# The low product of P moved behind the transposes of the next block, in attention with a two-layer FFN on one NeuronCore

## The chip, the cores and the metric

The kernel runs on one core of a Trainium2 chip. The metric is the device time of one execution in microseconds; the median of the runs counts. Names used below: PE is TensorE, DVE is VectorE, ACT is ScalarE, POOL is GpSimd, SP is SyncE, which issues all the DMAs.

## The reference

Inputs are q, k, v of 8 batches x 12 heads x 448 positions x 64, two vectors of gains, and the weights w_in (768 x 2048) and w_out (2048 x 768).

```
q_n, k_n = rmsnorm(q, g_q), rmsnorm(k, g_k)
attn = softmax(q_n @ k_n.T / sqrt(64))          # per batch and head, 448 x 448
x = (attn @ v) as 3584 x 768                    # heads side by side
h = x @ w_in
out = (h * cos(h)) @ w_out
```

## The kernel before, in words

Two heads of a batch make a unit: 48 units, `u` from 0 to 47. Units 0 to 5 (`u < NP`, called plain in the code) compute in float32. All others split their operands into a high part in the rounded type float32r and a low part, the rest, and add up the products high x high, low x high and so on, so that each product of 448 columns goes through PE in the faster type.

One unit from the seventh on goes like this.
- Scores: seven tiles of 128 queries, two or three matmuls each (`score`, L568). DVE scales and takes the row minimum (`rowmin`, L572), ACT takes the exponential and writes P, unnormalised, to SBUF (`expo`, L580). P has 11 slots of 448 columns; slots 0, 1 and 5 are used by every unit, the others by every second one.
- P has to be turned before it can be multiplied by v. `transp` does this on PE, in four blocks of keys, `kc` 0 to 3. Blocks 0 to 2 have two groups of transposes each, `part` 0 with four tiles into PSUM bank PT0 and `part` 1 with three tiles into PT1 (L614). Block 3 has 64 keys left for each head; three transposes (L619) turn a joint piece of both heads and one more (L621) turns tile 3, all into PT0, in one group. With block 1 goes a small transpose of the reciprocal row sums (L623).
- `pt_high` (ACT, L637) casts the bank to float32r, `hi`; `pt_low` (DVE, L644) subtracts and writes `lo`. In block 3 the low part goes into the other 64 partitions of `hi` (L646), so one product does both.
- `av` on PE multiplies for each of the two heads `hh`: the high product (L661) has as weights the high and the low part of v side by side, 128 columns; the low product (L663) has the high part of v alone, 64 columns. Both add to the PSUM bank `O{hh}` of the unit, which block 0 opens and block 3 closes.
- ACT and DVE copy and add the two halves of O (`x_half`, `x_sum`), POOL normalises (`x_norm`), and the result is split in high and low for the FFN.

The first FFN layer of a batch (`ffn1`, L745 to L747, six matmuls to a part, 48 parts for a batch) runs on PE between the attention of the next batch. Behind the attention comes the second layer (`ffn2`, L819 to L821), with some 470 us of its own.

The order of the work is planned when the kernel is built. Each piece is registered with `add(engine, cost, due, function, ..., r=keys read, w=keys written)`. The planner runs the pieces by their costs; on each engine, of the pieces whose inputs are there, the one with the smallest due time comes next. `dk` is the due time of a block, four units of planner time apart; a table shifts the due times by function (transposes of part 0 by -4.1, of part 1 by +2.4, `av` by +5.3). The costs only set the order. On the chip each engine works through its list in that order, and semaphores hold it where an input is missing. Keys such as `("lo", ...)`, `("pt", 0, half)` and `("O0", u)` stand for tiles and banks; `RING` gives how many buffers each name has: two each for `hi` and `lo`, one each for O0 and O1.

The product of a block in the code before, high and low one behind the other:

```
        nc.tensor.matmul(O, st, d["hi", kc][:, HEADS[hh]], start=(kc == 0), stop=(kc == 3))
        if kc < 3:
            nc.tensor.matmul(O[:D], vs[:, 0], d["lo", kc][:, HEADS[hh]], start=False, stop=False, skip_group_check=True)
```

Of the kernel before, what the change touches and what calls it, by code (L numbers as in the profile page):

```python
# [20 lines left out]
PE, ACT, DVE, POOL, SP = "PE", "ACT", "DVE", "POOL", "SP"  # L21
# [147 lines left out]
def tile_attention_moe(  # L169
# [11 lines left out]
    nc = tc.nc  # L181
    NU = sd_in.shape[0]
    B, S, D = 8, kq_in.shape[2] - 512, 64
    NP = NU // B
    NQT = 7
    NVC = 4
# [102 lines left out]
    stage, quad, part = {}, {}, {}  # L289
# [45 lines left out]
    pair = {}  # L335
# [20 lines left out]
    def p_key(u, t):  # L356
        slot = SLOTS[u % 2][TURNED[u % 2].index(t)]
        return (f"P{slot}", u if slot in (0, 1, 5) else u // 2)

    def p_slot(key):  # L360
        return int(key[0][1:])

    def p_rows(u, t):
        return pbuf[:, p_slot(p_key(u, t))]
# [236 lines left out]
    pt = [ps_t.tile([128, 512], F32, tag=f"PT{i}", name=f"PT{i}") for i in range(2)]  # L601
    TILES = ((0, 1, 2, 3), (4, 5, 6))
    COLS = (slice(0, 512), slice(512, 896))
    WIDE = (512, 384)
    HEADS = (slice(0, S), slice(S, 2 * S))
# [3 lines left out]
    def transp(u, kc, part, last):  # L609
        k = KS[kc]  # L610
        if kc < 3:
            for i, t in enumerate(TILES[part]):
                c = k + 64 * (t > 3)
                nc.tensor.transpose(pt[part][:, i * 128 : i * 128 + 128], p_rows(u, t)[:, c : c + 128], ident)  # L614
        else:
            flat = pbuf.rearrange("p n s -> p (n s)")
            for t in range(3):
                e = S * (p_slot(p_key(u, t)) + 1)
                nc.tensor.transpose(pt[0][:, t * 128 : t * 128 + 128], flat[:, e - 64 : e + 64], ident)  # L619
            c, n = (k - 64, 128) if u < NP else (k, 64)  # L620
            nc.tensor.transpose(pt[0][:n, 384:512], p_rows(u, 3)[:, c : c + n], ident)  # L621
        if last:
            nc.tensor.transpose(pt[1][:NQT, 384:512], pair[u]["sm"][:, 3, :], ident)  # L623

    def p_tile(u, kc, name, dt, part):
        if part == 0:
# [21 lines left out]
    def o_bank(u, hh):  # L648
        return pair[u]["O", hh]

    def o_open(u, hh):
        pair[u]["O", hh] = ps_o.tile([128, 512], F32, tag=f"O{hh}", name=f"O{u}_{hh}")

    def av(u, kc, hh):
        d = pair[u]
        if kc == 0:
            o_open(u, hh)
        O = o_bank(u, hh)[:, :S]
        vs = d["vs"][:, hh * NVC + kc]
        st = vs.rearrange("p a d -> p (a d)")  # L660
        nc.tensor.matmul(O, st, d["hi", kc][:, HEADS[hh]], start=(kc == 0), stop=(kc == 3))  # L661
        if kc < 3:
            nc.tensor.matmul(O[:D], vs[:, 0], d["lo", kc][:, HEADS[hh]], start=False, stop=False, skip_group_check=True)  # L663

    def pt_copy(u, kc, part):
        p = p_tile(u, kc, "hi", F32, part)
# [337 lines left out]
    def attend(u):  # L1004
        D0 = base(u)
        b, cc = divmod(u, NP)
        plain = u < NP
        step = 3.0 if plain else 4.0
        lead = 0.0 if u < NP else None
        def soften(t, n, key, due):  # L1010
            add(DVE, 0.65, due, rowmin, u, t, r=[("r", u)], w=[key, ("sm", u, 1, t)])
            add(ACT, 0.65, due + 1, expo, u, t, r=[key, ("sm", u, 1, t)], w=[p_key(u, t), ("sm", u, 2, t)])

        for j in range(4):
            if not plain:
                break
            tiles = (3,) if j == 3 else (j, j + 4)
            keys = [place(u, 2 * j + n) for n in range(len(tiles))]
            dj = D0 + step * j
            add(PE, 1.1 if j < 3 else 0.92, dj, score_plain, u, j, lead=lead, r=[("qp", u), km_key(u), ("xsb", 0)], w=keys)  # L1020
            for n, t in enumerate(tiles):
                soften(t, 2 * j + n, keys[n], dj + 1)
        for n, t in enumerate(TURNED[u % 2]):
            if plain:
                break
            key, dj = place(u, n), D0 + 0.5 * step * n
            if t == 3:
                r = [("qhi", u), ("ql", u), ("khi", u), ("kl", u)]
            else:
                r = [("D", u), ("E", u), ("M", u, 0), ("M", u, 1)]  # L1030
            add(PE, 0.62 if t == 3 else 0.41, dj, score, u, n, lead=lead, r=r, w=[key])
            soften(t, n, key, dj + 1)
        D1 = D0 + 4 * step
        add(ACT, 0.2, D1, rsum, u, 0, r=[("sm", u, 2, t) for t in range(7)], w=[("sm", u, 3)])
        add(DVE, 0.2, D1 + 1, rsum, u, 1, w=[("sm", u, 3)])
        for n, kc in enumerate((0, 1, 3, 2) if plain else range(4)):
            dk = D1 + step * n
            m = 4 * u + n
            turn = kc == KTURN
            for half in range(1 + (kc < 3)):  # L1040
                r = [p_key(u, t) for t in (TILES[half] if kc < 3 else range(7))]
                w = [("pt", 0, half)]
                last = turn and half == 1
                if last:
                    r.append(("sm", u, 3))
                if half and kc in (KTURN, KTURN + 1):
                    w.append(("pt", 0, 2))
                cost = (0.47, 0.36 + 0.11 * last)[half]
                add(PE, cost, dk, transp, u, kc, half, last, r=r, w=w, lead=lead)
            lows = []  # L1050
            for half in range(2):
                bank = ("pt", 0, half if kc < 3 else 0)
                keys = dict(r=[bank], w=[("hi", m, half)])
                if plain:
                    if kc < 3 or not half:
                        add((ACT, DVE)[half], (0.49, 0.42)[half], dk + 1, pt_copy, u, kc, half, **keys)
                else:
                    add(ACT, (0.52, 0.43)[half], dk + 1, pt_high, u, kc, half, **keys)
                if turn and half:
                    add(DVE, 0.28, dk + 1, rs_copy, u, r=[("pt", 0, 2), ("hi", m, 1)], w=[("rt", u)])  # L1060
                    add(SP, ISS, dk + 2, rs_store, u, r=[("rt", u)], w=[("rsd", u)], kb=4.0)
                if not plain:
                    l = 3 * u + kc
                    r, w = [bank], [("hi", m, half)]
                    if kc < 3:
                        r, w = r + w, [("lo", l, half)]
                    lows.append((half, r, w))
            for half, r, w in lows:
                if kc == 3:
                    r = r + [("hi", m, 1)]  # L1070
                add(DVE, (0.64, 0.5)[half], dk + 2, pt_low, u, kc, half, r=r, w=w)
            for hh in range(2):
                r = [("hi", m, half) for half in range(hh + 1)]
                if plain:
                    if kc < 3:
                        add(PE, 0.88, dk + 3, av_plain, u, kc, hh, lead=lead, r=[("vs", u)] + r, w=[(f"O{hh}", u)])
                    elif not hh:
                        add(PE, 1.3, dk + 3, av_plain, u, kc, hh, lead=lead, r=[("vs", u)] + r, w=[("O0", u), ("O1", u)])
                    continue
                if kc < 3:  # L1080
                    r += [("lo", l, half) for half in range(hh + 1)]
                add(PE, 0.41 if kc < 3 else 0.21, dk + 4, av, u, kc, hh, lead=lead, r=[("vs", u)] + r, w=[(f"O{hh}", u)])
        D2 = D1 + 4 * step + 1
        add(SP, 2 * ISS, D1 + 9, rs_load, u, r=[("rsd", u)], w=[("rs", u)], kb=224.0)
        for hh in range(2):
            if plain:
                add(DVE if hh else ACT, 0.55, D2, x_plain, u, hh, r=[(f"O{hh}", u)], w=[("xf", u, hh)])
                continue
            add(ACT, 0.54, D2, x_half, u, hh, r=[(f"O{hh}", u)], w=[("xf", u, hh)])
            add(DVE, 0.62, D2 + 1, x_sum, u, hh, r=[(f"O{hh}", u)], w=[("xf", u, hh)])  # L1090
        x = [("xf", u, 0), ("xf", u, 1)]
        add(POOL, 1.22, D2 + 5, x_norm, u, r=[("rs", u)], w=x)
        add(ACT, 0.46, ffn_due(b, 0) - 6, x_split, u, 0, r=x + ([] if b else [('xsb', 1)]), w=[("xs", cc, 0)])
        add(POOL, 1.11, ffn_due(b, 0) - 5, x_split, u, 1, r=x + [("xs", cc, 0)], w=[("xs", cc, 1)])
# [68 lines left out]
    add = plan.add  # L1163
# [3 lines left out]
    for fc in range(NEAR, NFC):  # L1167
        n = fc - NEAR
        d, y, he = BLOCK * n, ("y", n % 8), (("he", "he2")[n % 2], n // 2)
# [32 lines left out]
    for t in range(B // 2):  # L1202
# [26 lines left out]
        for k, (name, q, w0, bk, opens, closes) in enumerate(PRODUCTS):  # L1229
            d = DUE[name]  # L1230
# [5 lines left out]
            for g in range(NGR):  # L1236
# [6 lines left out]
                for o in range(3):  # L1243
                    add(PE, BLOCK / 3, e + BLOCK / 3 * o, ffn2, n, g, wpos, role[bk][o], o, opens,
                        r=[hk, lk] + [("wp", i) for i in wpos], w=[("y", role[bk][o])])
# [88 lines left out]
```

## Time and profile before

| | |
|---|---|
| median of 3 runs | 1373.1 us (1373.09 to 1374.74) |
| span of the profiled execution, first to last instruction | 1369.6 us |
| the execution's own time beside its span | not given by itself; the median of the runs is 3.5 us above the span |
| busy time in the span: PE, DVE, ACT, POOL | 1343.3, 1074.6, 926.7, 631.4 us |
| first and last low product (L663) | 109.5 and 889.5 us |

The profile is one execution on the chip. Times are microseconds, those marked ns nanoseconds. PE is the matmuls of TensorE, PEld its weight loads, which can overlap them. The start of a matmul is recorded, its end is modelled, and matmuls are pipelined, so an instruction of 0.37 us can be followed by the next one 0.20 us later. In an instruction's form, 128*64 means that 128 rows and 64 columns of the array are in use, that is, weights with 64 columns. L663 is line 663 of the kernel. An arrow names what ended the idle time before an instruction.

### The profile page before, as it was taken

What the parts mean: (1) busy time and instruction counts of PE and PEld (TensorE: products, weight loads), DVE (VectorE), ACT (ScalarE), POOL (GpSimd) and SP (SyncE); (2) the same over time, 40 slices, a digit from 0 to 9 for tenths busy, and PEclk for the clock granted to TensorE, in tenths of its full rate; (3) what the DMA queues carried; (4) which work ended last, traced back from release to release, by engine and by line L of the source; (5) the groups of instructions that cost most, each with busy time, mean ns of one, the idle gap of its engine ahead of it and who ended that gap; (6) DMA issues with size and microseconds to landing.
All of it is one profiled execution on the core that took longest, in us unless ns stands there. A gap on an engine that the chain in (4) does not pass through costs nothing.

```text
span 1369.6 us, 21501 instructions
## 1 busy us (share of the span) xinstructions
PE 1343.3 (98%) x6998; PEld 1172.3 (86%) x6998; DVE 1074.6 (78%) x1859; ACT 926.7 (68%) x1872; POOL 631.4 (46%) x554
## 2 busy tenths in 40 slices
PE   7899999999999999999999999999999999999998
PEld 3347888788888989888889888999999999999998
DVE  7898999977787887777877877628889889889743
ACT  6677888777877877777777787638567366366321
POOL 4889978676766866766776584330000000000000
PEclk9999999999999999999999999999999999999999
DMA  6898777889797898798987897338988368369334
GB/s 240 268 280 180 197 167 200 231 233 243 202 263 205 224 241 209 213 244 231 240 211 197 226 234 199 121 126 315 375 295 301 120 245 308 112 247 313 105 113 153
DMA packets 149472, 302.19 MB, mean 221 GB/s; under 512 B 34368, under 2 KB 83088, under 8 KB 149360
## 3 DMA queue, kind: packets, MB, share of 16 engines
q1 hardware_dynamic: 149360, 300.83, 75.4%
q8 instruction: 55, 0.90, 0.3%
q14 instruction: 57, 0.47, 0.1%
HBM read 193.99 MB, written 62.73 MB: 187 GB/s over the span
## 4 chain that ended last, share of the span: by engine, by line
PE 83%; DVE 6%; POOL 4%; DMA 3%; issue 2%; ACT 2%; SPq 0%; POOLq 0%; ACTq 0%; DVEq 0%
PE y L820 10%; PE y L819 10%; PE y L821 10%; PE ph L745 8%; PE ph L746 8%; PE ph L747 8%; PE S L568 7%; PE PT L614 6%; PE O L661 4%; PE O L663 3%; DVE S L572 1%; PE O L679 1%; PE S L552 1%; DVE lo L644 1%; PE y L747 1%
## 5 line engine op out<-in xcount | busy, mean ns | idle before, releaser
L572 DVE TENSOR_SCALAR_CACHE_REDUCE S<-S,r 128x448 f32<-128x448 f32 x336 | 225.2, 686 | 56.1 <-PE S L568 47.0
L580 ACT ACTIVATE P<-S,sm 128x448 f32<-128x448 f32 x336 | 213.4, 638 | 73.8 <-DVE S L572 56.3
L745 PE MATMUL ph<-xs,wi 128*128 128x448 f32 x660 | 251.1, 381 | 0.4 <-ACT hbuf L763 0.2
L819 PE MATMUL y<-g,wo 128*128 128x448 f32 x672 | 245.4, 365 | 0.0
L820 PE MATMUL y<-g,wo 128*128 128x448 f32 x672 | 245.4, 365 | 0.0
L821 PE MATMUL y<-g,wo 128*128 128x448 f32 x672 | 245.4, 365 | 0.0
L746 PE MATMUL ph<-xs,wi 128*128 128x448 f32 x660 | 241.8, 366 | 0.0
L747 PE MATMUL ph<-xs,wi 128*128 128x448 f32 x660 | 241.3, 366 | 0.0
L801 ACT CAST g<-gq 128x896 fp32r<-128x896 f32 x112 | 105.6, 943 | 169.8 <-PE y L821 169.4
L637 ACT CAST hi<-PT 128x512 fp32r<-128x512 f32 (+2 forms) x336 | 175.8, 533 | 64.1 <-PE PT L614 22.4
L644 DVE TENSOR_TENSOR lo<-PT,hi 128x512 fp32r<-128x512 f32 (+1 forms) x252 | 153.2, 619 | 39.7 <-ACT hi L637 37.6
L799 DVE TENSOR_TENSOR g<-gq,g 128x896 fp32r<-128x896 f32 x112 | 121.9, 1089 | 59.7 <-ACT g L801 59.2
L614 PEld LDWEIGHTS PT<-ident,P 128*128 128x128 f32 x1008 | 124.1, 141 | 41.9 <-issue 6.2
L614 PE MATMUL PT<-ident,P 128*128 128x128 f32 x1008 | 155.6, 275 | 2.9 <-DVE lo L644 1.2
L745 PEld LDWEIGHTS ph<-xs,wi 128*128 128x128 f32 x660 | 124.3, 188 | 16.4 <-ACT hbuf L763 2.0
L820 PEld LDWEIGHTS y<-g,wo 128*128 128x128 f32 x672 | 126.2, 188 | 10.0
L819 PEld LDWEIGHTS y<-g,wo 128*128 128x128 f32 x672 | 126.2, 188 | 9.9
L821 PEld LDWEIGHTS y<-g,wo 128*128 128x128 f32 x672 | 126.2, 188 | 9.9
L747 PEld LDWEIGHTS ph<-xs,wi 128*128 128x128 f32 x660 | 124.0, 188 | 10.6
L746 PEld LDWEIGHTS ph<-xs,wi 128*128 128x128 f32 x660 | 124.5, 189 | 8.7
L400 POOL TENSOR_TENSOR r<-r,nhalf 128x14 f32<-128x14 f32 (+1 forms) x48 | 124.1, 2586 | 4.0
L661 PE MATMUL O<-hi,vs 128*128 128x448 f32 x336 | 122.6, 379 | 1.1 <-DVE hi L646 0.9
(129 smaller groups left out, 2636.0 us busy)
## 6 DMA issues: line engine op xcount, KB each, us to landing
wo<-wo_d SPq DMA_DIRECT2D x152, 384.0 KB
gq<-h_d SPq DMA_DIRECT2D x64, 448.0 KB
h_d<-hbuf SPq DMA_DIRECT2D x54, 448.0 KB
wo_d<-ao SPq DMA_DIRECT2D x56, 384.0 KB
sd<-sd SPq DMA_DIRECT2D x46, 448.0 KB
kq<-kq SPq DMA_DIRECT2D x42, 480.0 KB
D<-qhi SPq DMA_DIRECT2D x84, 192.0 KB
raw<-w_in SPq DMA_DIRECT2D x16, 768.0 KB
```

The costliest lines, as they stand in the source:

```text
L572: nc.vector.tensor_scalar(d["S", t][:, :S], d["S", t][:, :S], d["r"][:, t : t + 1], None, op0=ALU.mult, op1=ALU.min, accum_out=d["sm"][:, ...
L580: nc.scalar.activation(p_rows(u, t), d.pop(("S", t))[:, :S], AF.Exp, bias=sm[:, 1, t : t + 1], scale=-1.0, accum_out=sm[:, 2, t : t + 1],)
L614: nc.tensor.transpose(pt[part][:, i * 128 : i * 128 + 128], p_rows(u, t)[:, c : c + 128], ident)
L637: nc.scalar.copy(hi if kc < 3 else hi[:64], pt_rows(u, kc, part))
L644: nc.vector.tensor_tensor(lo, src, hi.bitcast(F32), ALU.subtract)
L661: nc.tensor.matmul(O, st, d["hi", kc][:, HEADS[hh]], start=(kc == 0), stop=(kc == 3))
L745: nc.tensor.matmul(ph[:, :S], whi, x2[:, 0, :], start=(cc == 0), stop=False)
L746: nc.tensor.matmul(ph[:, :S], whi, x2[:, 1, :], start=False, stop=False)
L747: nc.tensor.matmul(ph[:, :S], wlo, x2[:, 0, :], start=False, stop=(cc == NCC - 1))
L819: nc.tensor.matmul(y, whi, hi[:, e], start=first and e == 0, stop=False, **more)
L820: nc.tensor.matmul(y, whi, lo[:, e], start=False, stop=False, **more)
L821: nc.tensor.matmul(y, wlo, hi[:, e], start=False, stop=last and e == NG - 1, **more)
```

## The change

The low product leaves `av`. It is issued as `av_low` at the end of `transp`: the group `part` of block `kc` ends with the low product of block `kc - 1` for head `part`. For block 3 `transp` is therefore called twice: part 0 has the three joint transposes, part 1 the transpose of tile 3, and each ends with a low product of block 2. The planner is told that these groups read `lo` of the block before and write the bank O, and gets new costs for them and for `av`. The first six units and their calls stay as they are.

```
-        else:
+        elif part == 0:
             flat = pbuf.rearrange("p n s -> p (n s)")
             for t in range(3):
...
+        if kc == 3 and (part or u < NP):
             c, n = (k - 64, 128) if u < NP else (k, 64)
             nc.tensor.transpose(pt[0][:n, 384:512], p_rows(u, 3)[:, c : c + n], ident)
         if last:
             nc.tensor.transpose(pt[1][:NQT, 384:512], pair[u]["sm"][:, 3, :], ident)
+        if u >= NP and kc:
+            av_low(u, kc - 1, part)
...
         nc.tensor.matmul(O, st, d["hi", kc][:, HEADS[hh]], start=(kc == 0), stop=(kc == 3))
-        if kc < 3:
-            nc.tensor.matmul(O[:D], vs[:, 0], d["lo", kc][:, HEADS[hh]], start=False, stop=False, skip_group_check=True)
+
+    def av_low(u, kc, hh):
+        vh = pair[u]["vs"][:, hh * NVC + kc, 0]
+        O = o_bank(u, hh)[:D, :S]
+        nc.tensor.matmul(O, vh, pair[u]["lo", kc][:, HEADS[hh]], start=False, stop=False, skip_group_check=True)
...
-            for half in range(1 + (kc < 3)):
-                r = [p_key(u, t) for t in (TILES[half] if kc < 3 else range(7))]
-                w = [("pt", 0, half)]
+            for half in range(1 + (kc < 3 or not plain)):
+                tiles = TILES[half] if kc < 3 else range(7) if plain else ((0, 1, 2, 4, 5, 6), (3,))[half]
+                r = [p_key(u, t) for t in tiles]
+                w = [("pt", 0, half if kc < 3 else 0)]
+                if kc and not plain:
+                    r += [("vs", u)] + [("lo", 3 * u + kc - 1, h) for h in range(half + 1)]
+                    w.append((f"O{half}", u))
...
                 cost = (0.47, 0.36 + 0.11 * last)[half]
+                if not plain and kc:
+                    cost = (0.43, 0.33 + 0.11 * last)[half] if kc < 3 else (0.32, 0.11)[half]
+                    cost += 0.15
                 add(PE, cost, dk, transp, u, kc, half, last, r=r, w=w, lead=lead)
...
-                if kc < 3:
-                    r += [("lo", l, half) for half in range(hh + 1)]
-                add(PE, 0.41 if kc < 3 else 0.21, dk + 4, av, u, kc, hh, lead=lead, r=[("vs", u)] + r, w=[(f"O{hh}", u)])
+                add(PE, 0.205, dk + 4, av, u, kc, hh, lead=lead, r=[("vs", u)] + r, w=[(f"O{hh}", u)])
```

## Rows read from the trace of the kernel before

**Rows 1.** The page: the span, and the chain that ended last by engine.
```profile
span 1369.6 us, 21501 instructions
...
PE 83%; DVE 6%; POOL 4%; DMA 3%; issue 2%; ACT 2%; SPq 0%; POOLq 0%; ACTq 0%; DVEq 0%
```
**Rows 2.** Stretches: length, busy time of the engines, granted clock, DMA share, GB/s.
```profile
100.00:250.00 150.00, 144.66 (x772) 122.83 (x771) 136.22 (x250) 118.32 (x268) 130.50 (x107) 0.99 0.76 188
250.00:895.00 645.00, 641.80 (x3549) 573.41 (x3548) 501.03 (x1067) 491.88 (x1153) 420.38 (x375) 1.00 0.83 218
895.00:1369.60 474.60, 470.74 (x2323) 435.99 (x2321) 353.78 (x368) 246.34 (x292) 9.58 (x9) 1.00 0.64 225
```
**Rows 3.** Groups by line and form: count, busy us, mean ns, idle before, releaser.
```profile
L663 PE MATMUL O<-lo,vs 128*64 128x448 f32 x252 | 92.7, 368 | 1.4 <-DVE lo L644 1.4
L661 PEld LDWEIGHTS O<-hi,vs 128*128 128x128 f32 x336 | 61.6, 189 | 12.5 <-DVE hi L646 1.7 <-issue 0.6 <-ACT sd L391 0.5
L663 PEld LDWEIGHTS O<-lo,vs 128*64 128x64 f32 x252 | 34.0, 135 | 5.7 <-DVE lo L644 2.1
```
**Rows 4.** One stretch, L663 alone: length, busy us of PE and PEld (count), clock, DMA.
```profile
100.00:250.00 150.00, 16.65 (x44) 6.10 (x44) 0.99 0.76 188
```
**Rows 5.** Timeline of PE, steady flow: start, duration, line, tiles, form, count.
```profile
499.76 0.37 PE L663 MATMUL O<-lo,vs 128*64 128x448 f32 x1
499.97 0.36 PE L661 MATMUL O<-hi,vs 128*128 128x448 f32 x1
500.17 0.37 PE L663 MATMUL O<-lo,vs 128*64 128x448 f32 x1
```
**Rows 6.** Timeline of weight loads behind a group of transposes.
```profile
503.26 0.19 PEld L745 LDWEIGHTS ph<-xs,wi 128*128 128x128 f32 x1
503.37 0.19 PEld L746 LDWEIGHTS ph<-xs,wi 128*128 128x128 f32 x1
```
**Rows 7.** Timeline of PE at the same place.
```profile
503.26 0.27 PE L614 MATMUL PT<-ident,P 128*128 128x128 f32 x1
503.29 0.45 PE L745 MATMUL ph<-xs,wi 128*128 128x448 f32 x1
503.58 0.36 PE L746 MATMUL ph<-xs,wi 128*128 128x448 f32 x1
```
**Rows 8.** Timeline of weight loads behind an idle gap.
```profile
117.62 0.19 PEld L568 LDWEIGHTS S<-M,D 128*128 128x128 f32 x1 [1.24 <-ACT P L580]
117.73 0.19 PEld L568 LDWEIGHTS S<-M,E 128*128 128x128 f32 x1
```
**Rows 9.** Timeline of PE behind two idle gaps, with 128 and with 64 columns.
```profile
117.62 0.47 PE L568 MATMUL S<-M,D 128*128 128x448 f32 x1 [1.00 <-ACT P L580]
117.93 0.37 PE L568 MATMUL S<-M,E 128*128 128x448 f32 x1
...
139.90 0.42 PE L663 MATMUL O<-lo,vs 128*64 128x448 f32 x1 [0.37 <-DVE lo L644]
140.16 0.49 PE L619 MATMUL PT<-ident,P 128*128 128x128 f32 x3
```
**Rows 10.** Timeline of weight loads within transposes, one of them with 64 columns.
```profile
513.43 0.11 PEld L621 LDWEIGHTS PT<-ident,P 128*64 128x64 f32 x1
513.54 0.36 PEld L614 LDWEIGHTS PT<-ident,P 128*128 128x128 f32 x3
```
**Rows 11.** Timeline of PE in one unit: transposes of blocks 2 and 3, a product.
```profile
491.82 0.60 PE L614 MATMUL PT<-ident,P 128*128 128x128 f32 x4
492.17 0.45 PE L661 MATMUL O<-hi,vs 128*128 128x448 f32 x1
...
495.45 0.49 PE L619 MATMUL PT<-ident,P 128*128 128x128 f32 x3
```
**Rows 12.** Timeline of weight loads in the float32 units, transposes and then L679.
```profile
68.63 0.14 PEld L614 LDWEIGHTS PT<-ident,P 128*128 128x128 f32 x1
68.94 0.19 PEld L679 LDWEIGHTS O<-hi,vs 128*64 128x64 f32 x2 [0.17 <-issue]
```

## The prediction

> **What bounds the kernel now.** I read the page first, then the stretches, then single instructions of TensorE. The page gives TensorE 83% of the chain that ended last, over a span of 1369.6 us [rows 1]; the reader should see that no other engine holds more than 6% of that chain. The stretches split this up [rows 2]: from 250 to 895 us TensorE is idle for 645.0 - 641.8 = 3.2 us, from 100 to 250 us for 150.0 - 144.7 = 5.3 us, and behind 895 us, where no product of P is left, for 3.9 us. The granted clock is 1.00 from 250 us on, so the upper of the two levels. VectorE and ScalarE have 501 and 492 of the 645 us. So between 100 and 895 us the time is the sum of the slots that TensorE's instructions take, one behind the other, plus at most 8.5 us of idle time. The change lies wholly in that part. A busy TensorE is not a TensorE at its peak, though, and the question is how long a slot is.
>
> A slot is the distance between two starts. In steady flow it is 0.20 to 0.21 us for a product of 448 columns, whether its weights have 64 columns (low part, L663) or 128 (L661) [rows 5]. A weight load lasts 189 ns for 128 columns and 135 ns for 64 [rows 3]; in steady flow it runs under the product before it, and the 54 ns of difference are worth nothing.
>
> **Where they could be worth something: behind a transpose.** A transpose takes only 0.11 us [rows 10]. Behind the last one of a group the weights of the next product start to load at 503.26 us, and the load behind that one can start only 0.11 us later, at 503.37 [rows 6]. The product itself was taken up at 503.29, 0.03 us behind the start of that load, and its successor came at 503.58, 0.29 us later and not 0.20 [rows 7]. That looks like a product that stands ready and waits for its weights. A place where nothing else can have been waited for gives the same numbers: after an idle gap the load at 117.62 us is followed by the next at 117.73, 0.11 us again [rows 8], and from its product to the next it is 117.93 - 117.62 = 0.31 us. The low product behind an idle gap (139.90, after a wait for VectorE) has 140.16 - 139.90 = 0.26 us, and the instruction lasts 0.42 us, not 0.47 [rows 9]. So a product with 64 columns of weights whose load is bare is 0.05 us shorter than one with 128.
>
> **The change, part by part.** Each of the 42 units from the seventh on has three blocks with a low product for two heads: 252 products [rows 3]. None is added or removed; the count of matmuls, loads, casts and transfers stays, and no DMA and no work of GpSimd or SyncE is moved past another by hand.
> - The low product moves from behind its high product to behind a group of transposes. There its load is bare, and it is the short one. Before, five of these six groups of a unit ended in a 128-column load (the last block had one group, now two). I take 0.05 us for each of the 252 places, the difference just read: 252 x 0.05 = 12.6 us. Bounds: 0 if the transpose itself and not the load holds the array for those 0.11 us (rival 1), 0.054 us by the durations of the loads [rows 3], 13.6 us.
> - The Trainium skill says in "TensorE: Matmul & The Clock Gate", section "LDWEIGHTS (loading the stationary operand)", that a load takes its columns divided by 1.2 in ns, which is 107 and 53. The bare load of 0.11 us agrees with the first; by that rule the sum would be an estimated 13.4 us.
> - The product behind the low one, formerly bare behind transposes, now loads under 0.20 us of product: no cost.
> - 44 of the 252 lie between 100 and 250 us (7.3 units at six each) [rows 4], where TensorE idles for other reasons and a shorter slot partly turns into more idle time. I count these by half: 22 x 0.05 = 1.1 us less, 11.5 us.
> - The wait for the low part (VectorE, L644) leaves the product. It is 1.4 us in all [rows 3]. The transposes of the next block had to wait for the same subtraction before, because they overwrite the bank it reads. So nothing new is waited for there; up to 1.4 us might go. I set this to nothing against the next item.
> - New order: the transposes of a block now come behind the high product of the block before, since both write the same O bank. Before, the first high product of a unit's block 0 stood at 492.17 us, behind the transposes of block 2 (491.82), and those of block 3 came at 495.45 [rows 11]. Block 1 must now come behind that product, so the transposes of blocks 1 to 3 slide back by more than one distance between blocks, 495.45 - 491.82 = 3.6 us. Queued behind them are casts, subtractions, and the exponentials of the next unit, which share three slots of P with this one. The cover is that TensorE has FFN products to fill with: idle time is 0.5% of the stretch from 250 us on. I set it to nothing; if the cover fails it is rival 2.
> - The split of the last block into two groups moves one transpose by at most one product; the cast of that block waits 0.2 us longer, under FFN products.
>
> The profiled execution spans 1369.6 us; the median of the three runs is 1373.1, and I take the 3.5 us between them as lying around the span and unchanged. Sum: 1369.6 - 11.5 + 3.5 = 1361.6 us. Work behind 895 us comes earlier and is no shorter.
>
> **The rivals.**
> 1. *The transpose holds the array.* From one transpose to the next it is 0.11 us even where the next weights have 64 columns: the load at 513.43 is followed by another at 513.54 [rows 10]. That speaks for an array that is occupied for 0.11 us whatever is loaded, and then the short load gains nothing. Against it: the FFN product was taken up 0.03 us behind the start of the last transpose [rows 7], where a following transpose is not. Only the 1.4 us of waits and about half of the 3.2 us of idle time are left to gain: 1370 to 1373.1 us.
> 2. *The new order starves TensorE (slower).* Place: the transposes of blocks 1 to 3 and the exponentials behind them. Price: where the units don't yet cover each other, from 100 to 250 us, TensorE loses 5.3 us in 7.3 units [rows 2, 4], 0.73 us each; at that rate 42 units lose 31 us, and 1361.6 + 31 is about 1392 us. It decides from 11.5 / 42 = 0.27 us a unit on. For it speaks that the order is set by due times that stay as they are; against it, that the FFN products fill 99.5% of the later stretch now.
> 3. *Going from 128-column to 64-column weights empties the array (slower).* A product of the first six units (L679, 64 columns, plain float32 operands) shows this behind transposes: its load starts at 68.94 us, 0.31 us behind that of the last transpose at 68.63, with 0.17 us idle [rows 12], where steady flow has 0.11. It is 0.20 us late; less the 0.05 us that the short load may give back this is 0.15 to 0.20 us at 252 places, 38 to 50 us: 1411 to 1423 us. The Trainium skill has the rule, "TensorEngine Tiling (Array Packing)", section "Key Properties": a change of tiling mode drains the engine. Against it: L661 and L663 alternate now between 128 and 64 columns at 0.20 to 0.21 us with no gap [rows 5], so the low product does not seem to switch anything.
>
> **How the numbers follow.** My forecast 0.64; rival 1 0.18; rival 2 0.11; rival 3 0.07. The predicted time is that of the likeliest: 1361.6 us. Its own range is 1355 (13.6 us, the 1.4 us of waits and the 3.2 us of idle time all gone) to 1367 (half lost to the new order). The whole range adds rival 1 and stops short of 2 and 3, which hold 0.18: 1354 to 1375 us. Runs of this kernel differ by 0.1%, and 0.2%, 2.7 us, is about what can be told from no change. Forecast and the better edge of rival 1 (0.04) are faster: 0.68. The rest of rival 1 is no change: 0.14. Rivals 2 and 3 are slower: 0.18.
>
> **What would show it.** In the profile after, the low product directly behind a transpose should have its successor 0.26 us after the start of its load (0.31 under rival 1; a gap before its load under rival 3). TensorE's idle time from 250 to 895 us should stay below 6 us; over 15 us says rival 2, and then the waits will name P, hi or S. The last product of attention, now before 895 us, should come some 11 us earlier and the stretch behind it keep its length. The prediction is wrong if either the slot is not shorter or the idle time grows by as much as it is.

## The result and the profile after

The kernel with the change takes 1387.6 us (median of 4 runs, 1385.4 to 1393.1), the kernel before, run beside it, 1373.1 us (4 runs, 1372.4 to 1374.7). The ratio is 1.0112, with a 95% interval of 1.009 to 1.0133: slower, where 1361.6 us and faster had been forecast. The span of the profiled execution grew from 1369.6 to 1385.7 us, by 16.1 us. The medians are only 14.5 us apart: a run takes some 2 us more than its span, so the traced execution of the kernel before was about 1.6 us shorter than the median. (The prediction had put all 3.5 us between the two around the span.)

The page of the kernel after: the span, and the chain that ended last, by engine.

```profile
span 1385.7 us, 21559 instructions
...
PE 79%; DMA 6%; POOL 4%; ACT 4%; DVE 3%; issue 2%; SPq 1%; POOLq 0%; ACTq 0%; DVEq 0%
```

Against [rows 1] TensorE lost four points of the chain, DMA gained three and ScalarE two. The stretches of the kernel after (columns as in [rows 2]; the last row is a narrower look at the place where the second layer begins):

```profile
100.00:250.00 150.00, 142.48 (x752) 120.52 (x751) 134.17 (x248) 116.87 (x266) 124.84 (x104) 0.99 0.73 183
250.00:895.00 645.00, 640.03 (x3524) 574.99 (x3522) 503.99 (x1054) 484.90 (x1143) 422.40 (x372) 1.00 0.85 216
...
960.00:985.00 25.00, 20.27 (x88) 17.93 (x87) 22.88 (x24) 17.72 (x25) 0.00 (x0) 0.86 0.86 305
```

The reader should look at the count as well as at the busy time. TensorE's idle time from 250 to 895 us grew by only 1.8 us (5.0 for 3.2), and from 100 to 250 us by 2.2 us; but 25 and 20 matmuls fewer were started in these stretches. The ends of matmuls are modelled, and an instruction is recorded as longer than its slot, so a wait shorter than some 0.16 us (0.37 of duration less 0.20 of slot) is not seen as idle time at all, and of every longer wait the first 0.16 us are missing.

A measure that sees it: for each matmul, the distance of its end from the end of the one before, less 0.203 us for a product of 448 columns or 0.109 us for a transpose (the slots of steady flow), summed from 110 us (where the plain float32 units are over) to the last product of attention. This **lost time in attention** is 19.2 us before and 27.6 us after. What grew are the longer waits: the places that lose more than 0.16 us add up to 15.1 us before (31 places) and 24.5 us after (51); in both kernels the slots of 3.4 us at the lower clock are among them.

With it the 16.1 us divide as follows.
- The last product of attention ends at 903.9 us instead of 892.7: 11.2 us later. Of this 8.4 us are lost time, and 2.2 us are first-layer work done earlier (from that product to the second layer it is 62.1 us instead of 64.3, so this part comes back). The remaining 0.6 us lie before 110 us.
- The second layer, from its first product to the end, takes 419.7 us instead of 412.6: 7.1 us more. At its start stands a stall that wasn't there before. Timeline of TensorE after, at that place:

```profile
971.53 0.74 PE L825 MATMUL y<-g,wo 128*128 128x448 f32 x1 [4.63 <-DMA wo<-wo_d]
972.07 0.57 PE L826 MATMUL y<-g,wo 128*128 128x448 f32 x1
972.44 0.57 PE L827 MATMUL y<-g,wo 128*128 128x448 f32 x1
...
976.55 0.47 PE L826 MATMUL y<-g,wo 128*128 128x448 f32 x1
976.86 0.37 PE L827 MATMUL y<-g,wo 128*128 128x448 f32 x1
```

  TensorE waits 4.63 us for weights of the second layer, and behind that its slots are 0.37 us instead of 0.20: the granted clock is at 0.5, the lower of its two levels, from 969.9 to 976.8 us (mean 0.86 in the window row above); it fell within the wait. Wait and clock together lose 7.3 us.

Why were the weights late? They are unpacked on the chip, split into two parts and stored (`v_store`, L332) in spare time during attention, and loaded again for the second layer. SyncE's queue, last stores and then the loads of `gq`, first before:

```profile
916.73 4.31 SPq L332 DMA_DIRECT2D wo_d<-ao  x2
...
921.13 4.69 SPq L776 DMA_DIRECT2D gq<-h_d  x9
```

and after:

```profile
924.25 17.03 SPq L332 DMA_DIRECT2D wo_d<-ao  x5
941.37 5.30 SPq L782 DMA_DIRECT2D gq<-h_d  x9
```

The last store starts at 941.0 us, 37.0 us behind the last product of attention, where before it was at 920.7, 28.0 us behind it (the rows give the stretch of several stores, which ends 0.3 us later). The first load of these weights follows at 949.8 us, before at 928.7. When attention ends, seven of the stores are still to come, where before there were four. The small jobs that lead to them have late due times and run between other work; what made them later in this order was not traced.

**The low product itself.** Timeline of TensorE after, at a block of the unit of [rows 11]:

```profile
492.01 0.60 PE L614 MATMUL PT<-ident,P 128*128 128x128 f32 x4
492.36 0.45 PE L669 MATMUL O<-lo,vs 128*64 128x448 f32 x1
492.65 0.36 PE L751 MATMUL ph<-xs,wi 128*128 128x448 f32 x1
```

and its weight loads:

```profile
492.34 0.14 PEld L669 LDWEIGHTS O<-lo,vs 128*64 128x64 f32 x1
492.45 0.19 PEld L751 LDWEIGHTS ph<-xs,wi 128*128 128x128 f32 x1
492.65 0.19 PEld L752 LDWEIGHTS ph<-xs,wi 128*128 128x128 f32 x1
```

The successor comes 492.65 - 492.34 = 0.31 us behind the start of the low product's load, not the forecast 0.26. That is the figure of rival 1, and the same 0.29 us from product to product as with 128 columns [rows 7]. There is no gap ahead of the load either, as rival 3 would have had it.

**Who waits.** Waits of TensorE (total us, times, longest), one of before, then after:

```profile
PE ph L745 <- ACT hbuf L763: 0.2, 1, 0.2
```

```profile
PE ph L751 <- ACT hbuf L769: 4.7, 8, 2.1
PE y L825 <- DMA wo<-wo_d: 4.6, 1, 4.6
...
PE O L664 <- DVE hi L649: 1.4, 2, 1.1
PE O L664 <- ACT hi L640: 1.2, 4, 0.5
```

Waits of ScalarE before, then after (its list is worked through in order, so what stands behind a waiting cast waits with it):

```profile
ACT P L580 <- DVE S L572: 56.3, 69, 2.6
ACT hi L637 <- PE PT L614: 22.4, 34, 1.8
ACT hi L637 <- PE O L661: 21.5, 25, 2.2
ACT hbuf L763 <- PE ph L747: 18.9, 38, 1.6
...
ACT P L580 <- PE PT L619: 11.8, 9, 1.9
```

```profile
ACT hi L640 <- PE PT L614: 45.0, 44, 3.4
ACT hbuf L769 <- PE ph L753: 40.9, 40, 2.6
ACT P L580 <- PE PT L619: 27.4, 24, 3.2
ACT P L580 <- DVE S L572: 22.8, 33, 2.5
```

The casts (`hi`) wait twice as long for transposes, which now stand behind the high product of the block before. But before, they waited another 21.5 us for high products, and after not at all. With two smaller rows of each kernel that are not shown (L621 to L624), their waits for TensorE are 55.1 us before and 56.4 after: the wait has changed its name and has hardly grown.

TensorE itself now waits for the copy of an FFN bank (`hbuf`): 0.2 us in all before, 4.7 after, in eight waits. What held the copies is mixed. The longest wait, 2.11 us, came behind a cast of q that had waited for GpSimd. Timeline of ScalarE, then of TensorE, at that place:

```profile
130.84 0.62 ACT L496 CAST qhi<-kq 128x512 fp32r<-128x512 f32 x1 [3.32 <-POOL kq L493]
131.36 0.54 ACT L769 ACTIVATE hbuf<-ph 128x448 f32<-128x448 f32 x1
```

```profile
131.95 0.47 PE L751 MATMUL ph<-xs,wi 128*128 128x448 f32 x1 [2.11 <-ACT hbuf L769]
```

Ahead of two more waits (0.36 and 0.31 us) the copy had itself waited for the store of an earlier copy, and ahead of one (0.63 us) a cast of P had waited 1.52 us for a transpose. The exponentials wait more than twice as long for the transposes that free their slots of P, but less for VectorE's scores (22.8 us, before 56.3), so the slots of P are no proof of a loss by themselves.

The idle time that this view shows in attention grew by 3.5 us, less than half of the 8.4; the rest lies in the first 0.16 us of each wait and in waits too short for this view. Counted from end to end, where more than 0.03 us is lost, TensorE loses 11.3 us ahead of first-layer products (1.7 before), 7.3 ahead of high products (2.7) and 3.3 ahead of transposes (5.7). So the loss lies mostly at the FFN products that were meant to fill the gaps, and no single wait makes it.

### The profile page after: what moved, and what is told of

Read it like the earlier page. It is cut to its first block, busy times and chain, and to the rows that moved or that the text cites. A ratio compares the mean times of both kernels' runs of the same rounds, so it can differ in the third digit from the quotient of the medians.

```text
span 1385.7 us, 21559 instructions
## 1 busy us (share of the span) xinstructions
PE 1352.2 (98%) x6998; PEld 1181.8 (85%) x6998; DVE 1085.9 (78%) x1859; ACT 924.9 (67%) x1872; POOL 635.1 (46%) x554
## 4 chain that ended last, share of the span: by engine, by line
PE 79%; DMA 6%; POOL 4%; ACT 4%; DVE 3%; issue 2%; SPq 1%; POOLq 0%; ACTq 0%; DVEq 0%
PE y L825 10%; PE y L826 10%; PE y L827 10%; PE ph L751 8%; PE ph L753 8%; PE ph L752 8%; PE S L568 7%; PE PT L614 6%; PE O L664 4%; PE O L669 3%; DMA h_d<-hbuf 2%; ACT P L580 1%; PE PT L619 1%; PE O L685 1%; DVE S L572 1%
## 5 line engine op out<-in xcount | busy, mean ns | idle before, releaser
L647 DVE TENSOR_TENSOR lo<-PT,hi 128x512 fp32r<-128x512 f32 x252 | 150.7, 618 | 36.4 <-ACT hi L640 34.3
L752 PEld LDWEIGHTS ph<-xs,wi 128*128 128x128 f32 x660 | 124.4, 188 | 10.5 <-POOL xs L735 0.7
```

The costliest lines, as they stand in the source:

```text
L647: nc.vector.tensor_tensor(lo, src, hi.bitcast(F32), ALU.subtract)
L752: nc.tensor.matmul(ph[:, :S], whi, x2[:, 1, :], start=False, stop=False)
```

## The experiments

The question after the result: is the gain of the short load real and more than eaten by the order, or is it not there? And does the order lose because of the new dependences, of the prices that the planner was given, or of due times that no longer fit? The kernel before, run beside each of the kernels below, took 1372.9 to 1374.1 us. Of each kernel one execution was traced. "Lost" is the lost time in attention as above (19.2 before, 27.6 after); "store" is how long after the last product of attention the last store of second-layer weights starts (28.0 before, 37.0 after).

**1. The low product with 128 columns of weights, same order** (both parts of v as weights, so it adds the low-by-low term that the kernel leaves out).

```
-        vh = pair[u]["vs"][:, hh * NVC + kc, 0]
-        O = o_bank(u, hh)[:D, :S]
+        vh = pair[u]["vs"][:, hh * NVC + kc].rearrange("p a d -> p (a d)")
+        O = o_bank(u, hh)[:, :S]
```

> The changed kernel, with 128 columns of weights (high and low part of v) instead of 64 in the low product behind the transposes; it adds the product of the two low parts, which the kernel leaves out otherwise. The order of all instructions stays that of the changed kernel. Theory A (the last transpose holds the array for 0.11 us, so the width of the next load is hidden): the time of the changed kernel within 3 us, 1385 to 1390 us, and the end of the low product 0.20 us behind that of the transpose as now. Theory B (the short load had saved 0.05 us at 252 places and something else lost more): 12.6 us longer, about 1400 us.

1391.7 us, ratio 1.0142 (1.0118 to 1.0167). Attention ends at 905.5 us, 1.6 us later than in the kernel after; lost 28.8. At 0.05 us for each of 252 products it would have been 12.6 us later. Timeline of TensorE in this kernel at the same block:

```profile
492.41 0.60 PE L614 MATMUL PT<-ident,P 128*128 128x128 f32 x4
492.77 0.45 PE L669 MATMUL O<-lo,vs 128*128 128x448 f32 x1
493.05 0.36 PE L751 MATMUL ph<-xs,wi 128*128 128x448 f32 x1
```

0.28 us from the low product to its successor, where 64 columns had 0.29. Over the 252 places the end of the low product is 206.3 ns on the mean (median 206) behind the end of the transpose, against 202.8 (median 202) with 64 columns. So the short load is worth at most 3.5 ns a place, 0.9 us in all. That is theory A, though the median lies 1.7 us above its range. Most of what the traced execution loses against the kernel after lies in the second layer (425.8 us for 419.7), where nothing was edited (experiment 5); it took 1396.5 us, 4.8 us above the median of this kernel.

**2. The old prices with the new order, and the new prices with the old order.** The first is the kernel after, the second the kernel before.

```
-                    cost = (0.43, 0.33 + 0.11 * last)[half] if kc < 3 else (0.32, 0.11)[half]
-                    cost += 0.15
+                    cost = (0.47, 0.36 + 0.11 * last)[half] if kc < 3 else (0.36, 0.11)[half]
+                    cost += 0.205
```
```
-                cost = (0.47, 0.36 + 0.11 * last)[half]
+                cost = (0.47, 0.36 + 0.11 * last)[half] if plain or not kc else (0.43, 0.33 + 0.11 * last)[half]
...
-                add(PE, 0.41 if kc < 3 else 0.21, dk + 4, av, ...
+                add(PE, 0.354 if kc < 3 else 0.21, dk + 4, av, ...
```

> The changed kernel, with the planner's old prices: 0.47 and 0.36 us for a group of transposes and 0.205 us for the low product at its end, instead of 0.43, 0.33 and 0.15; only the order of the lists can change. A unit then costs 5.94 planner us for transposes and products of P, as in the kernel before (5.95), and not 5.43. Theory P (the lists of ScalarE, SyncE and the rest are laid out for an attention some 22 us shorter than it is, so that they stand in a wrong order against TensorE): the wait of 5 us for the weights of the second layer goes and the lost slots of the attention go back to about 20 us, together 1371 to 1376 us. Theory O (the new dependences of the transposes on the high products do the harm): the wait at the second layer may go, but the attention keeps its 8 us, 1379 to 1384 us.

> The kernel before, with its code for TensorE as it was, but planner prices that make a unit as cheap as in the change: 0.43 and 0.33 us for the groups of blocks 1 to 3, 0.354 us for a pair of high and low product, 5.43 us for a unit. Theory P (prices): slower than before by most of what the change loses, 1380 to 1390 us, with the last store of split second-layer weights later against the end of attention. Theory O (dependences): 1372 to 1376 us.

Old prices, new order: 1386.8 us, 1.0114 (1.0079 to 1.0149), lost 25.1, store 37.1, and still a wait of 4.2 us for the second layer's weights. New prices, old order: 1383.8 us, 1.0091 (1.006 to 1.0122), lost 26.4, store 37.1. Nothing of what the second one executes differs from the kernel before but the order that the planner made of it, and its attention loses 7.2 us more than before, where the change loses 8.4. So another order, made by prices alone, is enough for such a loss; theory P had its time right (1380 to 1390 us). With the old prices the new dependences are enough too: 1386.8 us lies above both ranges, and the cure that theory P promised did not come. The waits are not the same ones: in the second kernel 7.6 us are lost ahead of transposes and 4.5 ahead of first-layer products (counted as above). What the two have in common is an order other than the one that the table of due times was made for. That this is the reason is a reading, which experiment 4 puts to a test.

**3. One due time.** If the transposes are held back by the high product, an earlier due time of `av` should help. The kernel after with `av` at -6.0 instead of +5.3, then the same with the low product priced at 0.205 us instead of 0.15; and, as a control, the kernel before with `av` at +5.0, a shift of 0.3 us.

```
-        "av": (5.3, 0.0, 0.0), ...
+        "av": (-6.0, 0.0, 0.0), ...
```

> The changed kernel with one number of the table of due times changed: the high product is due 6.0 us before its block's time and no longer 5.3 us after it, so that the transposes of the next block, which now come behind it, don't wait for a late due time. Prices as in the change. Theory D (the new dependence does harm only through that late due time: it holds the transposes, behind them the casts in ScalarE's list, and so the FFN's bank and the split of the second-layer weights): lost slots of the attention back to about 20 us from 28, no wait of 5 us in the second layer, 1370 to 1376 us. Theory O (the dependence itself, whatever the due time): attention as in the change, 1378 to 1388 us.

> The same as the one before, and the planner's price of a low product behind transposes is 0.205 us, what the trace of the changed kernel shows, instead of 0.15. Theory D: as the one before, with lists that fit TensorE a little better, 1369 to 1375 us. If wrong prices matter by themselves (theory P), this one is 3 us or more faster than the one before.

> The kernel before with the due time of its products (high and low) 0.3 us earlier, 5.0 instead of 5.3 in the table; nothing else. Theory T (the kernel before stands at a point that its table of due times was fitted to, and any other order loses the end of the split of second-layer weights behind the attention): 1376 to 1384 us, a wait for these weights when the second layer starts, last store of split weights more than 33 us behind the last product of attention instead of 28. Theory S (small changes of order are worth nothing, so that what the change lost is its own): 1371 to 1375 us.

Attention gained nothing: lost 27.7 and 30.2, last product at 904.0 and 903.9 us (903.9 after). The stores moved, to 19.6 us behind attention and to 1.7 us ahead of its end, and in both the stall at the start of the second layer is gone. The times are 1389.2 us, 1.0113 (1.0098 to 1.0128), and 1383.1 us, 1.0077 (1.006 to 1.0094). (The 6 us between them are no gain of the better price: they lie in the pace of the second layer, 420.3 and 412.3 us, experiment 5.) Theory D is refuted in both. So stall and attention are two losses that can be had apart, and the idea that one late product holds all back fell. The control: 1375.9 us, 1.002 (1.0008 to 1.0033), lost 18.3, store 35.5 and small stalls (2.7 us, in part for these weights), between the ranges of the two theories. A shift this small moves the stores by 7.5 us and leaves attention as it was.

**4. A table of due times fitted to the new dependences.** All three numbers of every function were searched anew with the planner's own end as the aim: once for the change with the old prices (`a5`), once for the change with its own transpose prices and 0.205 for the low product (`a6`), once for the kernel before (`b3`). The first lines of the tables before and of `a5`:

```
-        "av": (5.3, 0.0, 0.0), "av3": (3.6, 0.0, 0.0), "av_plain": (0.0, 0.0, 15.8), ...
+        "av": (5.9, -8.0, -13.9), "av3": (-6.1, -5.8, -22.0), "av_plain": (7.6, 3.1, 14.1), ...
```

> The changed kernel with the old prices and a table of due times that was fitted to its own dependences: the planner's list now ends TensorE at 916 planner us, as the list of the kernel before does (917), where the changed kernel with the same prices and the old table ended at 930. TensorE's instructions are those of the change, in another order. Theory T (the table was fitted to the order before, and that is all that the change lost): lost slots of the attention back to about 20 us, no wait at the second layer, 1370 to 1376 us. Theory O (the new dependences cost on the chip what the planner doesn't see): 1378 us or more.

> The changed kernel with prices as the traces show them (0.43 and 0.33 us for a group, 0.205 us for the low product at its end) and a table of due times fitted to these; TensorE's list ends at 914 planner us. Theory T: as the one before, 1368 to 1376 us. If lists without slack in TensorE's prices are bad by themselves, this one is some us slower than the one before.

> The kernel before with a table of due times fitted in the same way, from 917 to 914 planner us; nothing else. It is the measure for the two others: what such a table is worth without the change. Theory T: 1368 to 1375 us, and the fitted changed kernel within 3 us of it. Theory O: the same here, and the fitted changed kernels 6 us or more above it.

`a5` has all the dependences of the change, and its attention ends at 892.6 us (892.7 before), lost 15.4, store 5.9, no stall. (Its float32 units end 3.1 us later than before, so the smaller loss behind 110 us does not end attention earlier.) One of ScalarE's waits in it:

```profile
ACT hi L640 <- PE PT L614: 20.8, 32, 1.6
```

and the last store of SyncE's queue is over before the loads of `gq` begin:

```profile
898.52 0.42 SPq L332 DMA_DIRECT2D wo_d<-ao  x1
...
913.45 1.82 SPq L782 DMA_DIRECT2D gq<-h_d  x4
```

The casts wait 20.8 us for these transposes and 33.3 us for TensorE in all, less than before the change (55.1). So the new dependence does not force the loss. Theory T has attention and stall right. Still the time is 1378.0 us, 1.0026 (1.0016 to 1.0036), because the second layer takes 420.3 us, which neither theory had foreseen. The other two show that such a search is no recipe: `a6` 1389.3 us, 1.011 (1.0089 to 1.0131), attention until 900.2 us, lost 22.9; `b3` 1383.6 us, 1.0072 (1.0056 to 1.0088), until 896.7 us, lost 21.3. The planner's own end, at which the search aimed, does not tell which table is good on the chip. Theory T missed both times, by 13 and 9 us. So one fitted table shows that attention can be had back with the new dependences; that a table which no longer fits is what loses it is not shown, since a new fit cost the kernel before 4.0 us of attention.

**5. The 8 us of the second layer.** In `a3`, `a5`, `a6` and `b3` the second layer runs without a stall and yet takes 420.3 us, where before it was 412.6; in `a2` the same comes on top of a stall. Windows of TensorE alone over 400 us of it (length, busy us and count, clock, DMA share, GB/s), before:

```profile
960.00:1360.00 400.00, 400.00 (x1976) 1.00 0.65 227
```

and in `a5`:

```profile
960.00:1360.00 400.00, 400.00 (x1937) 1.00 0.64 221
```

Same clock, no idle time, and 39 products fewer: a slot of 206.7 ns instead of 202.7. In every kernel the pace stayed as it was from the last irregular place on, and such a place can be a wait: in `b1` the slot is 206.7 ns up to a wait at 969.6 us and 202.7 behind it; in `a2` it is 202.7 from 977 us on and 206.7 from 1006.4 us on, where TensorE loses 0.07 us. Could an irregular instruction change it? Three kernels on top of `a5` add transposes of the identity matrix into a bank that the next product overwrites: one in the first layer's last batch (`c1`), one for each output part in the second layer (`c2`), six in the first layer's last batch (`c3`).

```
+        if fc == NEAR:
+            nc.tensor.transpose(banks[bank][:, :128], ident, ident)
```
```
+            if first and o == 0:
+                nc.tensor.transpose(y[:, :128], ident, ident)
```
```
+        if fc > NEAR and fc % 2:
+            nc.tensor.transpose(banks[bank][:, :128], ident, ident)
```

> The changed kernel with its fitted table, and one more transpose of the identity, 0.11 us, in front of the FFN products that follow the attention; it goes into a bank that the next product overwrites. In the trace without it every product from there to the end takes 206.7 ns, in the kernel before 202.7. Theory L (TensorE falls into one of two steady paces behind the last irregular place and keeps it): the extra transpose can put it into the other pace; then all 2,300 products behind it are 4.0 ns shorter, 9 us, and the time is about 1369 us; if it falls back into the same pace, 1378 us. Rival M (the pace belongs to the program, its addresses or its layout): 1378 us and 206.7 ns.

> The same with the extra transposes in the second layer instead, one in front of each bank group that opens, 16 in all, 1.7 us. Theory L: the pace changes at one or more of these places within one execution, at the place of a transpose and nowhere else; 1371 to 1380 us by where it changes. Rival M: 206.7 ns from the first to the last product, 1380 us.

> The same with six extra transposes, one in front of every second block of FFN products behind the attention. Theory L: the pace may change at each, and the one behind the last holds for the second layer: about 1370 us or 1379 us. Rival M: 1379 us and 206.7 ns all the way.

`c1`: 1377.1 us, 1.0042 (1.0026 to 1.0057); the transpose changed nothing, the pace is 206.7 ns to the end. `c2`: 1376.6 us, 1.0032 (1.0019 to 1.0044); its transposes switch the pace in both directions, eleven of sixteen of them. Timeline of TensorE in `c2` at one that switches to the shorter slot:

```profile
969.28 0.37 PE L829 MATMUL y<-g,wo 128*128 128x448 f32 x1
...
969.90 0.36 PE L829 MATMUL y<-g,wo 128*128 128x448 f32 x1
970.11 0.27 PE L822 MATMUL y<-ident 128*128 128x128 f32 x1
970.13 0.45 PE L827 MATMUL y<-g,wo 128*128 128x448 f32 x1
970.42 0.36 PE L828 MATMUL y<-g,wo 128*128 128x448 f32 x1
...
971.02 0.37 PE L828 MATMUL y<-g,wo 128*128 128x448 f32 x1
971.23 0.36 PE L829 MATMUL y<-g,wo 128*128 128x448 f32 x1
```

From 969.28 to 969.90 three slots take 0.62 us (206.7 ns each), from 970.42 to 971.23 four take 0.81 (202.5). Two windows of `c2`, each 25 us without a switch, show the same in counts:

```profile
1137.00:1162.00 25.00, 25.00 (x125) 1.00 0.94 329
...
1197.00:1222.00 25.00, 25.00 (x123) 1.00 0.50 171
```

In these windows the share of DMA is higher where the slot is shorter, so traffic of the DMAs is not what makes it long. `c3` switched at its first transpose, at 924.8 us, and kept 202.7 ns to the end:

```profile
960.00:1360.00 400.00, 400.00 (x1976) 1.00 0.65 224
```

1370.1 us (median of 10 runs, 1368.4 to 1372.5), ratio 0.998 (0.9969 to 0.9992): the only one below the kernel before. Its second layer takes 412.3 us, 8.0 us less than in `a5`, for 2,016 products of 4.0 ns each (8.1 us). So the pace does not belong to the program as such (rival M): a transpose can set it. Whether it is the same in every execution of a kernel was not traced. The traced execution of `c3` is not shorter than that of before (1370.5 and 1369.6 us), but it took 2.4 us more than the median of its kernel. Whether the 0.2% come from the fitted table or from the change was not separated. The slots of the low product, as measured in experiment 1, give no more than 0.9 us of it.

## Why the prediction was wrong

**"252 x 0.05 = 12.6 us": this step failed, and the whole forecast of a gain rested on it.** The term is at most 0.0035 x 252 = 0.9 us. (By the prediction's own words only five of six places, 210 in all, had a bare load to lose, so that its sum should have been 10.5 us.) The two numbers it came from, a bare load of 0.11 us for 128 columns and an end 0.05 us earlier for 64 [rows 8, 9], are right for a product behind an idle gap (in `b1` one more with 64 columns is followed by a product after 0.25 us, those with 128 after 0.31). Behind a transpose they don't apply, because there the load isn't what the product waits for: the transpose holds the array for 0.11 us, whatever is loaded beside it. [Rows 10] said so, as rival 1 put it: a 64-column load is followed at 0.11 us too. What was set against it, the FFN product taken up 0.03 us behind the start of the last transpose [rows 7], is no evidence: with 64 columns the record looks the same (0.02 us behind its load, successor at 0.31). I read a start that the hardware records early as a product that stands ready.
The Trainium skill's rule in "TensorE: Matmul & The Clock Gate", section "LDWEIGHTS (loading the stationary operand)", that a load takes time in proportion to its columns, is not contradicted by this: behind idle gaps the rows agree with it. But a price of the load gives no gain where something else as long runs beside it, and the sum by the rule (13.4 us) failed with mine.

**"New order: I set it to nothing": this step failed too, and it made the kernel slower.** It was named as rival 2. Its cover, FFN products to fill with, held only in part: 8.4 us were lost in attention, 0.2 us a unit, where the start-up rate that I took for the price gave 0.73. The path that rival 2 names, late transposes and the casts behind them, is not shown: the casts wait 56.4 us for TensorE, before 55.1. What shows is that the cover itself waits: first-layer products stand 4.7 us for their bank, whose copies were held by several things. And with no gain on the other side, no threshold of 0.27 us a unit was left to reach. The runs add what rival 2 lacked: the loss is not forced by the dependences (`a5` has them, and its attention ends at 892.6 us), and another order made by prices alone causes it (`b1`). That the due times fit other numbers is the likeliest reason, but only one of the two tables fitted to the change bears it out; what in the order costs the 8.4 us stays open.

**"The stretch behind keeps its length": wrong by 4.9 us.** The second layer took 7.1 us more, and 2.2 us of first-layer work had been done earlier. The prediction did not follow the preparation of the second layer's weights, which is due late. In the new order it ended later, and the second layer waited 4.63 us for weights that are loaded behind its last store. A loss in attention alone does not do that: `a3` and `a4` lose as much there, and the stall is gone.

**Right:** rival 3 does not happen; the low product's load follows the last transpose after 0.11 us. The rule of the Trainium skill that a change of tiling empties the engine ("TensorEngine Tiling (Array Packing)", section "Key Properties") does not show at these float32r products, if 64 columns of weights are such a change at all. The wait for `lo` did leave the low product, as the group by line and form shows (count, busy us, mean ns, idle before):

```profile
L669 PE MATMUL O<-lo,vs 128*64 128x448 f32 x252 | 110.3, 446 | 0.0
```

It is 0.0 us of idle time where [rows 3] had 1.4. (The mean of 446 ns for 368 is the early start of the record behind a transpose, not a longer slot.) The half for the start-up and the split of the last block were too small for any run to test.

**The test of 6 us of idle time** was badly chosen: 5.0 us would have passed it, while 25 matmuls were missing from the stretch.

## What to carry to other kernels

A price read behind an idle gap is not the price behind another instruction: look for the row with the same neighbour first (here a 64-column load within transposes). Where an order is planned from costs and fitted due times, a change of dependences or of prices by a few hundredths of a microsecond can cost 1% by itself, so a change should be judged with more than one order, each tried on the chip: here one of the two tables fitted to the change gave attention its time back. On an engine that is nearly always busy count the instructions of a stretch, since waits shorter than the overlap of two matmuls are no idle time in the records and longer ones are counted short by it; and follow the work that is due late too, as its last transfer may open the next stage.

## What the runs showed of the hardware

- Products of 448 columns with a weight load each run at one of two steady paces, 202.7 or 206.7 ns, at the same granted clock of 1.00 and with no idle time. The pace stays until something irregular comes; a single transpose can switch it either way, and not every one does (eleven of sixteen in `c2`, the one in `c1` not); in `b1` and `a2` a wait switched it. Over the 2,016 products of the second layer this is 8 us, 0.6% of the kernel, as much as the whole loss in attention. What decides which pace follows stayed open.
- A transpose of 128 x 128 in float32 takes 0.11 us of TensorE whether the next load has 64 or 128 columns; the end of the product behind it comes 202.8 or 206.3 ns later (252 places each, `after` and `a2`).
